# Two attention steps behind one logits stretch, a third room for turned keys and queries, and a state started one step earlier

## The chip, the cores and the metric

The kernel runs on one core of a Trainium2 chip. The metric is device time in microseconds, the median of several runs of one program. Engines are named PE (TensorE, with PEld for its weight loads), DVE (VectorE), ACT (ScalarE), POOL (GpSimd) and SP (SyncE, which issues the DMAs).

## What is computed

Three layers in a row, all in float32: retention attention over 8 batches, 8 heads, 576 positions and head size 64; a gated feed-forward layer over the 4608 tokens of width 512 (hidden width 2048); and a soft mixture of 8 experts with 4 slots each.

```python
scores = scale * np.matmul(q, k.transpose(0, 1, 3, 2))
gamma = 1.0 - 2.0 ** (-5.0 - np.arange(H, dtype=np.float32))
Dmat = np.where(rel >= 0, gamma[:, None, None] ** rel[None, :, :], 0.0)
x = np.matmul(scores * Dmat[None], v)              # attention, then heads side by side
...
h = x @ w_in
x = (h * (1.0 / (1.0 + np.exp(-1.702 * h)))) @ w_out
...
logits = x @ phi                                   # softmax over tokens: d, over slots: c
slot_out[e] = np.maximum((d.T @ x)[e] @ w1[e], 0.0) @ w2[e]
out = c @ slot_out
```

## The kernel before

**Attention steps.** A step g (0 to 35) is one chunk of 64 positions of two sequences for all eight heads; nine steps (NPB) finish a pair of sequences, and cb = g % 9 is the chunk's number. Attention is done in the chunked form: a running state St gathers keys times values, and the output of a chunk is its state times the queries plus its masked scores times its values. `products(g)` writes the step's TensorE work as 64x64 matmuls, two at a time for the lower and the upper half of the partitions. Its out products are 32 matmuls (SS with QT and VN with SC, into Op; 16 of them where cb is 0, since there is no state yet). Its own products are 16 for the state (KN with VN, into St; none where cb is 8) and 16 for the next step's scores (KT with QT of g + 1, into Sp). Own and out products are written alternately, so that one own pair and one out pair run side by side: a slot. DVE then makes SC out of Sp (`scale_scores`) and SS out of St (`scale_state`) for the next step, and xs out of Op (`scale_out`); ACT rounds xs into x (`x_high`), POOL takes the remainder (`x_low`) and scales the keys KN (`scale_keys`).

**Packs.** A step's turned keys KT, keys KN, turned queries QT and values VN come by one DMA of 1 MB into a pack, which also has room for SC and SS. From step 3 on two packs are used in turn, and `load_step(g + 2)` is issued at the end of step g.

**Blocks.** The feed-forward runs over 12 blocks of 384 tokens (three steps each), in 16 chunks fc of 128 hidden columns: `expert_scores` writes 12 matmuls into hp, ACT makes gT by a gelu, DVE transposes it into pre, SP shuffles pre by 16 small DMAs into nat. The second matrix of the feed-forward is folded into the logits: `logits_group` multiplies four chunks of gT with Wp into Lg. The softmax over tokens runs in pieces (`softmax_split` into Lp, `softmax_exp` with lt, `softmax_turn` with dp), and `slots_part` sums the slots (Sg).

**Order.** Every engine's queue is written by hand. The list START gives blocks 0 and 1 with steps 0 to 8. Blocks n = 2 to 10 are a loop, in which `step_of` puts the three steps of block n + 1 behind chunks 3, 9 and 13 of block n (12 for n = 9; chunks 0, 3 and 6 for n = 10); `between` puts logits groups of the block before behind the step of chunk 3, and of this block behind the step of chunk 9. So on TensorE the loop reads: chunk 3, a step, Lg, chunk 4, lt, chunks 5 and 6, dp, chunks 7 to 9, a step, Lg, Sg, chunks 10 to 13, a step, chunks 14 to 3 of the next block. After the last step the pool of packs closes (`att_ctx.close()`) and four rooms of 1 MB for expert weights open in its place (`pw2`); two expert units (`kept`) load in block 3 into rooms of `ring_raw`. Block 11 and the tail (expert layers and output) follow.

Of the kernel before, what the change touches and what calls it, by code (L numbers as in the profile page):

```python
# [9 lines left out]
F32 = mybir.dt.float32  # L10
# [8 lines left out]
B, H, S, D = 8, 8, 576, 64  # L19
# [7 lines left out]
C = 64  # L27
NPB = S // C
NP = H // 2
# [3 lines left out]
LAST = NBLK - 1  # L33
# [9 lines left out]
NSEQ = 2  # L43
CP = NSEQ * C
NSTEP = NT // CP
# [22 lines left out]
STEP_AT = {3: 0, 9: 1, 13: 2}  # L68
BEFORE_EARLY_STEP_AT = {3: 0, 9: 1, 12: 2}
LOGITS_AT = {3: ((1, 2), (1, 3)), 9: ((0, 0), (0, 1))}  # L70
SPLIT_AT, EXP_AT, TURN_AT, SLOTS_AT = 3, 4, 6, 9
EARLY_STEP_AT = {0: 0, 3: 1, 6: 2}
# [61 lines left out]
def tile_kernel(ctx, tc, qkv, w_in, w_turned, w_out, phi, w1, w2, consts, out):  # L134
# [42 lines left out]
    KT, KN, QT, VN, SC, SS = range(6)  # L177
# [3 lines left out]
    packs.update({g: packs[(g - 3) % 2] for g in range(3, NSTEP)})  # L181

    def load_step(g):
        sp.dma_start(packs[g].rearrange("p c a j d -> p (c a j d)")[:, 0:4 * PC], qkv[g])

# [11 lines left out]

    def products(g, parts=("out", "state", "score")):

        n, cb = g + 1, g % NPB  # L200
        own, out_ = [], []
        if "out" in parts and g >= 0:
            t = packs[g]
            Op = Ops[g] = ps.tile([128, NP, NSEQ, C], F32, tag="r", name="Op", bufs=3)
            for p, j in pairs:
                if cb:
                    out_.append((Op, t, SS, QT, p, j, True))
                out_.append((Op, t, VN, SC, p, j, cb == 0))
        if "state" in parts and g >= 0 and cb < NPB - 1:
            if cb == 0:  # L210
                St[g // NPB] = ps.tile([128, NP, NSEQ, D], F32, tag="St", name="St")
            own += [(St[g // NPB], packs[g], KN, VN, p, j, cb + p + j == 0) for p, j in pairs]
        if "score" in parts and n < NSTEP:
            Sp = Sps[n] = ps.tile([128, NP, NSEQ, C], F32, tag="r", name="Sp", bufs=3)
            own += [(Sp, packs[n], KT, QT, p, j, True) for p, j in pairs]
        for i in range(max(len(own), len(out_))):
            for what, turn in ((own, 0), (out_, 1)):
                if i < len(what):
                    o, w, a, b, p, j, first_ = what[i]
                    for h, oh in ((lo, (lo, hi)[turn]), (hi, (hi, lo)[turn])):  # L220
                        pe.matmul(o[oh, p, j, :], w[h, a, p, j], w[h, b, p, j], start=first_, stop=True,  # L221
                                  skip_group_check=True)
# [31 lines left out]
    def step_of(g, between):  # L254
        products(g)
        scale_keys(g + 1)
        scale_scores(g + 1)
        scale_state(g + 1)
        between()
        scale_out(g)  # L260
        x_high(g)
        x_low(g)
        if g + 2 < NSTEP:
            load_step(g + 2)
# [292 lines left out]
    def again():  # L557
# [11 lines left out]
        "A": products, "B": lambda i: products(i - 1, ("score",)), "P": lambda i: products(i, ("out", "score")),  # L569
# [247 lines left out]
    with tc.manual_schedule(engines={getattr(mybir.EngineType, e) for e in ("PE", "Activation", "DVE", "Pool", "SP")}):  # L817
        for x in START:
            step(x)
        for n in range(2, LAST):  # L820
# [3 lines left out]
                (STEP_AT if n < LAST - 2 else BEFORE_EARLY_STEP_AT, LOGITS_AT, SPLIT_AT, EXP_AT, TURN_AT, SLOTS_AT))  # L824
            for fc in range(NFC):
# [39 lines left out]
                if n == 3 and fc == 0:  # L865
                    for unit, a in zip(kept, (4, 8)):
                        load_unit(unit, lambda a=a, n=len(unit): ring_raw[:, a:a + 2 * n].rearrange("p a f -> p (a f)"))
# [76 lines left out]
```

## Time and profile before

| | |
|---|---|
| time, median of 3 runs | 653.29 us (652.22 to 653.52) |
| span of the profiled execution | 649.8 us |
| PE busy in it | 628.7 us, 97% |
| DVE, ACT, POOL busy | 292.9, 217.3, 77.8 us |
| DMA moved | 150.64 MB, mean 232 GB/s |

The span runs from the first to the last instruction of one profiled execution; the time of a run is some microseconds longer. Busy PE is modelled, since matmuls are pipelined: lengths of stretches are better taken as differences of starts. Each matmul of the code is two entries of PE in the profile, the feed-forward ones and those of lt excepted, which are one.

### The profile page before, as it was taken

To read this page: it belongs to the slowest core of one execution; us is meant where nothing else is said; L and a number is where in the kernel's file an instruction comes from. 1 tells how busy PE (TensorE), PEld (TensorE's weight loads), DVE (VectorE), ACT (ScalarE), POOL (GpSimd) and SP (SyncE) were. 2 spreads that over 40 slices of the span, in tenths; PEclk is the share of its full clock that TensorE was granted. 3 is DMA by queue.
4 is the path that set the end of the run, shared out by engine and by line. 5 is a ranking of instruction groups with operands and counts; after the bars stand their busy time and mean duration, and the time that the engine had idled before them with its cause. 6 is when DMAs were issued, how large, how long until landed. Compare 5 with 4: busy or idle time off the path is not lost.

```text
span 649.8 us, 19162 instructions
## 1 busy us (share of the span) xinstructions
PE 628.7 (97%) x8439; PEld 540.2 (83%) x8439; DVE 292.9 (45%) x581; ACT 217.3 (33%) x409; POOL 77.8 (12%) x70
## 2 busy tenths in 40 slices
PE   5999999999999999999999999999999999999994
PEld 5898887898989989989989979989898798874562
DVE  3989933463454443444534533534535323123043
ACT  2774432141242332412412412412424224231042
POOL 2021102111111102111111011111121100001000
PEclk9999999999999999999999999999999999999998
DMA  8987666886687647646566657466566778989998
GB/s 338 405 326 284 238 150 178 208 197 160 178 286 191 177 157 181 190 143 180 168 166 181 190 133 192 165 157 172 183 178 184 265 200 213 414 332 422 414 418 361
DMA packets 62546, 150.64 MB, mean 232 GB/s; under 512 B 8192, under 2 KB 42368, under 8 KB 53248
## 3 DMA queue, kind: packets, MB, share of 16 engines
q1 hardware_dynamic: 62464, 149.43, 72.3%
q8 instruction: 66, 1.08, 0.7%
q14 instruction: 16, 0.13, 0.1%
HBM read 101.16 MB, written 13.63 MB: 177 GB/s over the span
## 4 chain that ended last, share of the span: by engine, by line
PE 87%; DMA 5%; DVE 3%; ACT 2%; issue 1%; POOL 0%; SPq 0%; DVEq 0%; ACTq 0%
PE hp L359 56%; PE Lg L410 5%; PE Sg L470 4%; PE St L221 4%; PE Sp L221 4%; DMA early_raw<-in_moe_w_in_dram 3%; PE Op L221 3%; PE h_ps L701 2%; PE op L778 2%; PE so_ps L752 1%; DMA early_raw<-in_w_turned_dram 1%; PE so_ps L744 1%; DMA pack<-in_qkv_dram 1%; PE tpg L392 1%; DVE early_raw L299 1%
## 5 line engine op out<-in xcount | busy, mean ns | idle before, releaser
L359 PE MATMUL hp<-x,w 128*128 128x384 f32 x2304 | 420.0, 339 | 1.6 <-POOL x L251 1.3
L359 PEld LDWEIGHTS hp<-x,w 128*128 128x128 f32 x2304 | 397.4, 188 | 20.1 <-issue 15.7
L385 DVE STREAM_TRANSPOSE pre<-gT 128x384 f32<-128x384 f32 x172 | 95.3, 569 | 167.8 <-ACT gT L369 159.7
L369 ACT ACTIVATE gT<-hp 128x384 f32<-128x384 f32 x188 | 91.3, 491 | 229.9 <-PE hp L359 229.4
L251 POOL TENSOR_TENSOR x<-xs,x 128x512 fp32r<-128x512 f32 x33 | 42.6, 1290 | 319.0 <-ACT x L246 319.0
L221 PE MATMUL Op<-pack 64*64 64x64 f32 x2176 | 71.5, 220 | 0.6 <-issue 0.6
L221 PEld LDWEIGHTS Op<-pack 64*64 64x64 f32 x2176 | 66.4, 135 | 1.0 <-issue 1.0
L246 ACT CAST x<-xs 128x512 fp32r<-128x512 f32 x36 | 22.3, 620 | 87.2 <-DVE xs L239 87.2
L227 POOL TENSOR_TENSOR pack<-pack,cs 128x512 f32<-128x512 f32 x30 | 32.3, 1076 | 119.3 <-DMA pack<-in_qkv_dram 74.7
L221 PE MATMUL Sp<-pack 64*64 64x64 f32 x1152 | 40.9, 221 | 5.8 <-DMA pack<-in_qkv_dram 5.8
L221 PEld LDWEIGHTS Sp<-pack 64*64 64x64 f32 x1152 | 37.5, 137 | 7.4 <-DMA pack<-in_qkv_dram 5.8
L231 DVE TENSOR_TENSOR pack<-Sp,cs 128x512 f32<-128x512 f32 x36 | 24.7, 687 | 36.7 <-PE Sp L221 19.0
L221 PEld LDWEIGHTS St<-pack 64*64 64x64 f32 x1024 | 32.9, 136 | 8.2 <-issue 8.1
L221 PE MATMUL St<-pack 64*64 64x64 f32 x1024 | 37.3, 223 | 0.1
L410 PE MATMUL Lg<-gT,Wp 128*32 128x384 f32 x376 | 36.3, 493 | 0.6 <-DVE Lall L457 0.5
L470 PE MATMUL Sg<-nat,dn 128*32 128x512 f32 x264 | 30.4, 593 | 0.0
L239 DVE TENSOR_TENSOR xs<-Op,cs 128x512 f32<-128x512 f32 x36 | 24.5, 682 | 3.4 <-PE Op L221 3.4
L295 ACT ACTIVATE early_raw<-early_raw 128x512 f32<-128x512 f32 x28 | 18.9, 688 | 12.5 <-DMA early_raw<-in_w_turned_dram 7.5
L235 DVE TENSOR_TENSOR pack<-St,cs 128x512 f32<-128x512 f32 x32 | 21.8, 681 | 2.7 <-PE St L221 1.6
L470 PEld LDWEIGHTS Sg<-nat,dn 128*32 128x32 f32 x264 | 8.4, 110 | 17.1 <-issue 17.1
L476 DVE SCALAR_TENSOR_TENSOR acc<-acc,corr,Sg 128x512 f32<-128x512 f32 x10 | 7.5, 747 | 28.3 <-PE Sg L470 28.3
L410 PEld LDWEIGHTS Lg<-gT,Wp 128*32 128x32 f32 x376 | 9.6, 109 | 12.1 <-issue 9.1
(142 smaller groups left out, 385.5 us busy)
## 6 DMA issues: line engine op xcount, KB each, us to landing
pack<-in_qkv_dram SPq DMA_DIRECT2D x36, 1024.0 KB, 5.5
nat<-pre SPq DMA_DIRECT2D x352, 96.0 KB, 2.3
wx<-in_moe_w_dram SPq DMA_DIRECT2D x19, 1024.0 KB, 8.4
ring<-in_moe_w_out_dram SPq DMA_DIRECT2D x16, 512.0 KB, 3.7
early_raw<-in_moe_w_in_dram SPq DMA_DIRECT2D x15, 512.0 KB, 6.3
early_raw<-in_w_turned_dram SPq DMA_DIRECT2D x13, 512.0 KB, 7.8
wx<-in_moe_w_dram SPq DMA_DIRECT2D x11, 512.0 KB, 13.8
out_dram<-wx SPq DMA_DIRECT2D x5, 1024.0 KB, 6.1
```

Of the source, the lines that this page charges most:

```text
L221: pe.matmul(o[oh, p, j, :], w[h, a, p, j], w[h, b, p, j], start=first_, stop=True, skip_group_check=True)
L227: (dve if n in (3, 4) else pool).tensor_tensor(k, k, by_state(ksc[:, n % NPB, :]), op=ALU.mult)
L231: dve.tensor_tensor(packs[n][:, SC], Sps.pop(n), across(dtab), op=ALU.mult)
L235: dve.tensor_tensor(packs[n][:, SS], St[n // NPB], by_state(stsc[:, n % NPB, :]), op=ALU.mult)
L239: dve.tensor_tensor(xss[g], Ops.pop(g), across(osc), op=ALU.mult)
L246: act.copy(xh[b_][:, :, i * CP:(i + 1) * CP], xss[g].rearrange("p a j c -> p a (j c)"))
L251: (eng or pool).tensor_tensor(xl[b_][:, :, cols_], xss.pop(g).rearrange("p a j c -> p a (j c)"), xh[b_][:, :, cols_], op=ALU.subtract)
L359: pe.matmul(hp, wt[fc][:, a, dc, :], b[n][:, dc, :], start=(i == 0), stop=(i == 3 * NDC - 1))
L369: act.activation(gT[n, g][:, fl, :], hps.pop((n, fc)), AF.Gelu_apprx_sigmoid)
L385: dve.transpose(pre[n, hf][:, :, :, fh, :].rearrange("p c b i -> p (c b) i"), gT[n, g][:, fl, :].rearrange("p (x j) -> p x j", j=32))
L410: pe.matmul(Lg[n][32 * fl:32 * fl + 32, :], Wp[:, g * GF + fl, :], gT[n, g][:, fl, :], start=(g == 0), stop=(g == NFC // GF - 1))
L470: pe.matmul(Sg[32 * b:32 * b + 32], dn[n][:, c, :], nv[:, 4 * b:4 * b + 4], start=(c == 0), stop=(c == NT128 - 1))
```

## The change

The three steps of a block now stand in two places. Behind chunk 3 (chunk 0 in block 10), `two_steps` writes the first step, the logits groups, and the second step right behind them; behind chunk 9 (chunk 3 in block 10), `third_step` writes the third. For this, the scores of step g + 2 are computed while step g + 1's queries and step g's room are still in use, so the turned keys and queries get three rooms in rotation: those of the two packs and `third`, in `ring_raw[:, 8:10]`. A pack's load is split in two halves of 512 KB (`load_turned`, `load_natural`), and the input is laid out so that each half is contiguous. From step 8 on scores come ahead of the state among the own products, and the Sp buffer is taken ahead of Op. The state products of a step with cb = 0 (9, 18 and 27) are written into the step before it, which has no state products of its own. The kept unit that lay in `ring_raw[:, 8:10]` from block 3 on now loads in block 10, and the four rooms of `pw2` open behind chunk 3 of block 10 and not behind chunk 6.

```diff
-STEP_AT = {3: 0, 9: 1, 13: 2}
-BEFORE_EARLY_STEP_AT = {3: 0, 9: 1, 12: 2}
+STEP_AT = {3: 0, 9: 2}
...
-EARLY_STEP_AT = {0: 0, 3: 1, 6: 2}
+EARLY_STEP_AT = {0: 0, 3: 2}
...
-    KT, KN, QT, VN, SC, SS = range(6)
+    KT, QT, KN, VN, SC, SS = range(6)
...
+    third = ring_raw[:, 8:10].rearrange("p c (a j d) -> p c a j d", a=NP, j=NSEQ)
+
+    def turned_room(g):
+        if g < NPB:
+            return packs[g][:, 0:2]
+        return (packs[3][:, 0:2], third, packs[4][:, 0:2])[(g - NPB) % STEPS]
...
+    def load_turned(g):
+        if g < NSTEP:
+            sp.dma_start(turned_room(g).rearrange("p c a j d -> p (c a j d)"), qkv[g][:, 0:2 * PC])
+
+    def load_natural(g):
+        if g < NSTEP:
+            sp.dma_start(packs[g][:, 2:4].rearrange("p c a j d -> p (c a j d)"), qkv[g][:, 2 * PC:4 * PC])
...
+        if "state" in parts and g >= 0 and (g == 0 or 0 < cb < NPB - 1):
+            state = states(g)
+        elif "state" in parts and cb == NPB - 1 and 0 <= g < NSTEP - 1:
+            state = states(n)
+        if g < NPB:
+            new_scores()
+        own = state + score if g < NPB - 1 else score + state
...
-    def step_of(g, between):
+    def step_products(g, between):
         products(g)
-        scale_keys(g + 1)
         scale_scores(g + 1)
         scale_state(g + 1)
         between()
+
+    def step_x(g):
         scale_out(g)
         x_high(g)
         x_low(g)
-        if g + 2 < NSTEP:
-            load_step(g + 2)
+
+    def two_steps(g, between):
+        step_products(g, between)
+        products(g + 1)
+        step_x(g)
+        scale_scores(g + 2)
+        scale_state(g + 2)
+        step_x(g + 1)
+        load_natural(g + 2)
+        load_turned(g + 3)
+        load_natural(g + 3)
+        load_turned(g + 4)
+        scale_keys(g + 2)
+        scale_keys(g + 3)
+
+    def third_step(g, between):
+        step_products(g, between)
+        step_x(g)
+        load_natural(g + 2)
+        load_turned(g + 3)
+        scale_keys(g + 2)
...
                 if fc in step_at:
-                    step_of((n + 1) * STEPS + step_at[fc], between)
+                    (third_step if step_at[fc] else two_steps)((n + 1) * STEPS + step_at[fc], between)
...
+                    load_unit(kept[1], lambda: ring_raw[:, 8:10].rearrange("p a f -> p (a f)"))
```

PE, end of step 18 and what follows it, in block 5 (chunk 3). Names end in numbers that tell buffers apart; x2 is the lower and the upper half of one product. Before:

```order
L221 MATMUL St<-pack_93 64x64 x2
L221 MATMUL Op<-pack_93 64x64 x2
L221 MATMUL Sp<-pack_92 64x64 x16
L410 MATMUL Lg<-gT,Wp 32x384 x8
L359 MATMUL hp<-x,w 128x384 x12
L423 MATMUL lt<-Lp,sum4r 128x384 x2
```

After:

```order
L250 MATMUL Sp<-ring 64x64 x2
L250 MATMUL Op<-pack_92 64x64 x2
L459 MATMUL Lg<-gT,Wp 32x384 x8
L250 MATMUL Sp<-pack_93 64x64 x2
L250 MATMUL Op<-ring,pack_93 64x64 x2
```

The 16 unpaired Sp matmuls are gone, since the state products that stood beside Op are in step 17 and the scores stand there now; and step 19 begins right behind Lg, where chunk 4 stood.

DVE, around chunk 3 of block 6, from the transposes of the chunks ahead of it on. Before:

```order
L385 STREAM_TRANSPOSE pre<-gT 128x12x32 x5
L231 TENSOR_TENSOR pack_92<-Sp,cs 128x512
L235 TENSOR_TENSOR pack_92<-St,cs 128x512
L417 TENSOR_TENSOR Lp<-Lg,Lp 128x384
L239 TENSOR_TENSOR xs<-Op,cs 128x512
L385 STREAM_TRANSPOSE pre<-gT 128x12x32
L425 TENSOR_REDUCE mb<-lt 128x1
```

After:

```order
L434 STREAM_TRANSPOSE pre<-gT 128x12x32 x5
L260 TENSOR_TENSOR pack_92<-Sp,cs 128x512
L264 TENSOR_TENSOR pack_92<-St,cs 128x512
L466 TENSOR_TENSOR Lp<-Lg,Lp 128x384
L268 TENSOR_TENSOR xs<-Op,cs 128x512
L260 TENSOR_TENSOR pack_93<-Sp,cs 128x512
L264 TENSOR_TENSOR pack_93<-St,cs 128x512
L268 TENSOR_TENSOR xs<-Op,cs 128x512
L434 STREAM_TRANSPOSE pre<-gT 128x12x32
L474 TENSOR_REDUCE mb<-lt 128x1
```

SC, SS and xs of the second step now stand between xs of the first and the transpose of chunk 4.

SP, the loads of one block of the loop, from the weights' load ahead of chunk 3 on. Before:

```order
L281 DMA ring<-in_moe_w_out_dram 128x1024
L184 DMA pack_93<-in_qkv_dram 128x2048
L342 DMA wo_dram<-ring 128x512
L281 DMA ring<-in_moe_w_out_dram 128x1024
L184 DMA pack_92<-in_qkv_dram 128x2048
L403 DMA nat<-pre 32x3x256 x16
L184 DMA pack_93<-in_qkv_dram 128x2048
```

After:

```order
L330 DMA ring<-in_moe_w_out_dram 128x1024
L200 DMA pack_93<-in_qkv_dram 128x1024
L196 DMA pack_92<-in_qkv_dram 128x1024
L200 DMA pack_92<-in_qkv_dram 128x1024
L196 DMA ring<-in_qkv_dram 128x1024
L391 DMA wo_dram<-ring 128x512
L330 DMA ring<-in_moe_w_out_dram 128x1024
L200 DMA pack_93<-in_qkv_dram 128x1024
L196 DMA pack_93<-in_qkv_dram 128x1024
L452 DMA nat<-pre 32x3x256 x16
```

Three loads of 1 MB became six of 512 KB, four behind the pair and two behind the third step.

## Rows read from the trace of the kernel before

**Rows 1.** The page: head, and shares of the chain that ended last.

```profile
span 649.8 us, 19162 instructions
...
PE 87%; DMA 5%; DVE 3%; ACT 2%; issue 1%; POOL 0%; SPq 0%; DVEq 0%; ACTq 0%
```

**Rows 2.** Two blocks: stretch, length, busy by engine (instructions), clock, DMA share, GB/s.

```profile
296.58:342.71 46.13, 46.13 (x638) 41.33 (x637) 20.47 (x39) 14.58 (x27) 7.00 (x6) 1.00 0.62 172
...
250.47:296.58 46.11, 46.11 (x574) 41.31 (x573) 19.64 (x38) 14.69 (x27) 6.99 (x6) 1.00 0.63 173
```

**Rows 3.** Timeline of PE, one block: start, length, engine, line, operation, tiles, shapes, count.

```profile
298.61 12.75 PE L359 MATMUL hp<-x,w 128*128 128x384 f32 x72
311.29 0.27 PE L221 MATMUL St<-pack 64*64 64x64 f32 x2
...
313.32 1.50 PE L410 MATMUL Lg<-gT,Wp 128*32 128x384 f32 x16
314.75 2.38 PE L359 MATMUL hp<-x,w 128*128 128x384 f32 x12
316.97 0.51 PE L423 MATMUL lt<-Lp,sum4r 128*128 128x384 f32 x2
...
328.17 0.27 PE L221 MATMUL St<-pack 64*64 64x64 f32 x2
...
334.19 8.59 PE L359 MATMUL hp<-x,w 128*128 128x384 f32 x48
342.71 0.27 PE L221 MATMUL St<-pack 64*64 64x64 f32 x2
```

**Rows 4.** Timeline of PE, steps 17 (from 250.47) and 18 (from 265.18).

```profile
250.47 0.27 PE L221 MATMUL Sp<-pack 64*64 64x64 f32 x2
...
251.41 1.16 PE L221 MATMUL Op<-pack 64*64 64x64 f32 x34
252.50 12.75 PE L359 MATMUL hp<-x,w 128*128 128x384 f32 x72
265.18 0.27 PE L221 MATMUL St<-pack 64*64 64x64 f32 x2
...
266.16 1.10 PE L221 MATMUL Sp<-pack 64*64 64x64 f32 x32
267.19 1.50 PE L410 MATMUL Lg<-gT,Wp 128*32 128x384 f32 x16
```

**Rows 5.** Timeline of PE in the start: Lg ahead of a step, hp behind one.

```profile
59.61 0.85 PE L410 MATMUL Lg<-gT,Wp 128*32 128x384 f32 x8
60.39 0.27 PE L221 MATMUL St<-pack 64*64 64x64 f32 x2
...
93.69 2.35 PE L359 MATMUL hp<-x,w 128*128 128x384 f32 x12
95.88 0.49 PE L452 MATMUL dp<-ident,dT 128*128 128x128 f32 x3
```

**Rows 6.** Timeline of DVE around the step at 311.29; in brackets idle before, and releaser.

```profile
311.99 0.58 DVE L385 STREAM_TRANSPOSE pre<-gT 128x384 f32<-128x384 f32 x1 [1.56 <-ACT gT L369]
313.42 0.69 DVE L231 TENSOR_TENSOR pack<-Sp,cs 128x512 f32<-128x512 f32 x1 [0.86 <-PE Op L221]
314.03 0.68 DVE L235 TENSOR_TENSOR pack<-St,cs 128x512 f32<-128x512 f32 x1
```

**Rows 7.** Timelines of SP and POOL in block 3: a load and its keys.

```profile
179.97 0.64 SPq L184 DMA_DIRECT2D pack<-in_qkv_dram  x1
189.43 1.04 POOL L227 TENSOR_TENSOR pack<-pack,cs 128x512 f32<-128x512 f32 x1 [9.24 <-DMA pack<-in_qkv_dram]
```

**Rows 8.** Stretches of the last 120 us, columns as in rows 2.

```profile
530.00:550.00 20.00, 19.51 (x123) 17.30 (x123) 7.45 (x16) 8.37 (x15) 0.00 (x0) 1.00 0.75 187
...
580.00:640.00 60.00, 56.97 (x780) 31.11 (x781) 19.52 (x53) 17.10 (x41) 2.80 (x3) 1.00 1.01 408
640.00:650.00 10.00, 1.14 (x14) 0.87 (x9) 1.68 (x4) 1.16 (x4) 0.00 (x0) 0.69 0.77 316
```

More of the change, by code (lines that the diff above doesn't have):

```diff
@@ L181, in tile_kernel, with plane @@
     packs.update({g: packs[(g - 3) % 2] for g in range(3, NSTEP)})
+    third = ring_raw[:, 8:10].rearrange("p c (a j d) -> p c a j d", a=NP, j=NSEQ)
[3 more added lines that the diff above has]
+        return (packs[3][:, 0:2], third, packs[4][:, 0:2])[(g - NPB) % STEPS]
+    def plane(g, c):
+        return turned_room(g)[:, c] if c in (KT, QT) else packs[g][:, c]
     def load_step(g):
         sp.dma_start(packs[g].rearrange("p c a j d -> p (c a j d)")[:, 0:4 * PC], qkv[g])
+    def load_turned(g):
[4 more added lines that the diff above has]
+            sp.dma_start(packs[g][:, 2:4].rearrange("p c a j d -> p (c a j d)"), qkv[g][:, 2 * PC:4 * PC])
     St, Sps, Ops, xss = {}, {}, {}, {}
@@ L196, in tile_kernel, with states, new_scores @@
     pairs = [(p, j) for p in range(NP) for j in range(NSEQ)]
+    def states(g):
+        k = g // NPB
+        if k not in St:
+            St[k] = ps.tile([128, NP, NSEQ, D], F32, tag="St", name="St")
+        return [(St[k], g, KN, VN, p, j, g % NPB + p + j == 0) for p, j in pairs]
     def products(g, parts=("out", "state", "score")):
         n, cb = g + 1, g % NPB
-        own, out_ = [], []
+        out_, state, score = [], [], []
+        def new_scores():
+            if "score" in parts and n < NSTEP:
+                Sps[n] = ps.tile([128, NP, NSEQ, C], F32, tag="r", name="Sp", bufs=3)
+                score.extend((Sps[n], n, KT, QT, p, j, True) for p, j in pairs)
+        if g >= NPB:
+            new_scores()
         if "out" in parts and g >= 0:
-            t = packs[g]
             Op = Ops[g] = ps.tile([128, NP, NSEQ, C], F32, tag="r", name="Op", bufs=3)
@@ L206, in products @@
                 if cb:
[L207 to L215, printed above, removed]
+                    out_.append((Op, g, SS, QT, p, j, True))
+                out_.append((Op, g, VN, SC, p, j, cb == 0))
+        if "state" in parts and g >= 0 and (g == 0 or 0 < cb < NPB - 1):
[3 more added lines that the diff above has]
+        if g < NPB:
+            new_scores()
+        own = state + score if g < NPB - 1 else score + state
         for i in range(max(len(own), len(out_))):
@@ L220, in products @@
                     for h, oh in ((lo, (lo, hi)[turn]), (hi, (hi, lo)[turn])):
-                        pe.matmul(o[oh, p, j, :], w[h, a, p, j], w[h, b, p, j], start=first_, stop=True,
+                        pe.matmul(o[oh, p, j, :], plane(w, a)[h, p, j], plane(w, b)[h, p, j], start=first_, stop=True,
                                   skip_group_check=True)
@@ L568, in tile_kernel @@
         "ac": lambda i: join(f"O{i}", ring[:, i % 4]), "e": wp_product, "ed": wp_turn,
-        "A": products, "B": lambda i: products(i - 1, ("score",)), "P": lambda i: products(i, ("out", "score")),
+        "U": load_turned, "V": load_natural, "A": products, "B": lambda i: products(i - 1, ("score",)), "P": lambda i: products(i, ("out", "score")),
         "Q": lambda i: products(i, ("out",)), "R": lambda i: products(i, ("state",)),
@@ L823, in tile_kernel @@
                 (EARLY_STEP_AT, EARLY_LOGITS_AT, EARLY_SPLIT_AT, EARLY_EXP_AT, EARLY_TURN_AT, EARLY_SLOTS_AT) if early else
-                (STEP_AT if n < LAST - 2 else BEFORE_EARLY_STEP_AT, LOGITS_AT, SPLIT_AT, EXP_AT, TURN_AT, SLOTS_AT))
+                (STEP_AT, LOGITS_AT, SPLIT_AT, EXP_AT, TURN_AT, SLOTS_AT))
             for fc in range(NFC):
@@ L865, in tile_kernel @@
                 if n == 3 and fc == 0:
-                    for unit, a in zip(kept, (4, 8)):
-                        load_unit(unit, lambda a=a, n=len(unit): ring_raw[:, a:a + 2 * n].rearrange("p a f -> p (a f)"))
+                    load_unit(kept[0], lambda: ring_raw[:, 4:8].rearrange("p a f -> p (a f)"))
         n = LAST
@@ L930 @@
     q, k, v = inputs["q"], inputs["k"], inputs["v"]
-    side = lambda h: np.concatenate([turned(k, h), rows(k, h), turned(q, h), rows(v, h)], axis=2)
+    side = lambda h: np.concatenate([turned(k, h), turned(q, h), rows(k, h), rows(v, h)], axis=2)
     host = {"qkv": np.ascontiguousarray(np.concatenate([side(1), side(0)], axis=1)), **host}
```

4 rows, old and new, of the table START are left out of this document.

## The prediction

> **What bounds the kernel now.** The head of the page and its chain come first: of a span of 649.8 us the chain of waits gives 87% to PE and 5% to DMA [rows 1]. The table by stretches comes next. One block of the steady loop, from one third attention step to the next, takes 46.13 us, and PE is busy for all of it at a granted clock of 1.00, while VectorE has 20.47 us of work, ScalarE 14.58, GpSimd 7.00, and the DMA engines a share of 0.62 [rows 2]. So whatever leaves PE's row there leaves the span, as long as nothing else becomes late. The second row is the telling one: the block with steps 17 and 18 has 574 matmul entries instead of 638 and lasts 46.11 us [rows 2]. Sixty-four entries fewer bought nothing: in a step the reader must count slots, not matmuls. The PE timeline gives the lengths of all stretches as differences of starts [rows 3], and the two odd steps stand in [rows 4].
>
> **Part 1, the removed stretch.** Before, nine blocks (n = 2 to 10) enter attention three times; after, twice, and the second step stands between the logits Lg and the next feed-forward chunk. Feed-forward matmuls hp run at a fixed pace: 48 after Sg take 8.52 us up to the third step, 72 after that step 12.68 [rows 3], so 24 more cost 4.16, or 0.1733 each. Before, the stretch from Sg to the next block's first step is 8.52 + one step + 12.68, so 21.20 without the step. After, it is one run of 120: 8.52 + 72 x 0.1733 = 21.00. That returns 0.20. The moved step itself keeps its length. It now follows Lg: the only Lg followed by a step in the trace is in the start, eight entries in 60.39 - 59.61 = 0.78 us [rows 5]. Sixteen entries up to hp take 314.75 - 313.32 = 1.43 [rows 3]; eight more for 0.65, so the end of an Lg run costs 0.13 in both cases and the join costs nothing extra. The chunk after the pair now follows a step, not Lg: 12 such matmuls take 95.88 - 93.69 = 2.19 [rows 5] against 316.97 - 314.75 = 2.22 [rows 3], 0.03 more back. Sum: 0.23 x 9 = 2.1 us. Bounds: nothing, if Lg to step is dearer inside the loop, and 3.3 us if the whole entry and exit vanished (a step is 16 slots of 0.117, 1.87, in a stretch of 2.03 [rows 4], so 0.16, and with the 0.20 of the hp side 0.36 x 9). I take 2.1, because each of its terms has a row of the same neighbours.
>
> Changing from hp to a step shows as a gap: the last hp starts a step late by about half a pace. The Trainium skill, "TensorEngine Tiling (Array Packing)", Key Properties, says that changing the tiling mode drains TensorE. By that rule one counts changes of shape: eight in a block before, seven after, since Lg to step is still one. At 0.1 us each this would give 0.9 us in place of 2.1 and a time of 649.9. The rows are nearer to 2.1, because a change costs on both sides of it.
>
> **Part 2, the state one step early.** Step 17 ends in 34 unpaired Op entries, 251.41 to 252.50, step 18 in 32 unpaired Sp entries, 266.16 to 267.19 [rows 4]. Both steps last as long as a full one: 252.50 - 250.47 = 2.03 and 267.19 - 265.18 = 2.01 [rows 4]. The other steps pair every own product with an out product, 16 slots; at (2.03 - 0.16) / 16 a slot is 0.117 us. After, the 16 state matmuls of step 18 fill the empty half of step 17's slots at no time, and step 18 has 8 slots in place of 16: 8 x 0.117 = 0.93. The same holds for steps 8 and 9 and 26 and 27, so 3 x 0.93 = 2.8 us. Bound below: step 17 could grow, if paired slots were slower than single ones; [rows 4] excludes it, since paired halves and single halves have the same length.
>
> **Part 3, what the second step waits for.** It needs SC and SS of its own step, which VectorE makes out of the first step's products. Before, the first step starts at 311.29, the third chunk's transpose ends at 311.99 + 0.58 = 312.57, SC begins at 313.42 and SS ends at 314.03 + 0.68 = 314.71 [rows 6]. The second step would start where hp starts now, at 314.75 [rows 3]: in time by 0.04. After, scores come first in the slots, so SC can run while the state is still multiplied, and only SS remains for the time after the step; then 0.6 us are spare. In the shortened steps 9, 18 and 27 the second step starts 0.93 earlier: the transpose ends 1.28 after the step's start, SC and SS take 1.29 (313.42 to 314.71), so 2.57 plus some hundredths, against 2.03 - 0.93 + 1.43 = 2.53. I charge 0.1 for each, 0.3 in all; between 0 and 0.6. On VectorE the softmax's Lp stays ahead of the moved work. Queued behind that work are xs of both steps and the fourth chunk's transpose, and behind xs on ScalarE the gelu of the fourth chunk. These come later by the same 2.03 us as the chunk itself.
>
> **Part 4, loads and keys.** Each load of 1 MB becomes two halves; bytes stay. The natural half of step g+2 is issued after the pair's first step, then SP issues three more halves, and GpSimd scales g+2's keys (1.04 us) after two xl instead of one. The third step wants these keys in its second half: 2.03 + 1.43 + 2.03 + 2.19, then 328.17 - 316.97 = 11.20 for lt, five chunks and dp [rows 3], so 18.9 us after the first step's start, and 0.9 more. The slowest load of the loop was issued at 179.97 and its keys began at 189.43, 9.5 us later [rows 7]. From 5.5 us (the pair's length) that lands at 15, plus 1.04 for the keys: 16, against 19.8. Nothing is charged.
>
> **Part 5, the end.** DMA share is 1.01 from 580 to 640 and 0.77 after [rows 8], so the weights and outputs of the tail fill the DMA engines. But the stretch before has a share of 0.75 [rows 8]: there is no backlog going in, and each tail load waits for a room that PE empties. A PE that comes earlier pulls them along. The half megabyte of kept weights that now loads in block 10, and four rooms that fill three chunks earlier, fall into that open stretch. Nothing is charged.
>
> **The sum.** 2.1 + 2.8 - 0.3 = 4.6 us. The span of 649.8 becomes 645.2. The three runs have a median of 653.29, 3.5 above the span; this remainder is launch and end, which the change doesn't touch. So 648.7 us.
>
> **The rivals.**
> - Only the slots pay: the joins cost what the removed stretch returns, and SS is late in each pair. For it: 0.04 us of spare time before the reordering. Against it: [rows 5]. 2.8 - 0.3 = 2.5, so 650.8.
> - The tail holds the end: its DMA work doesn't move with PE, and the gain turns into waiting there. For it: 1.01 over 60 us [rows 8]. Against it: the open stretch before. It would give 652 to 653.3, no change.
> - More than the sum: the 0.36 per stretch of the upper bound, and one of the small stalls of block 2 gone. 2.1 becomes 3.3, no charge for SS: 6.1, so 647.2.
> - Slower: keys of the third step late. It decides when the natural half lands more than 13.3 us after issue (19.8 - 5.5 - 1.0); each microsecond beyond it stops PE in eight blocks (2 to 9). To eat 4.6 it takes 0.6 beyond, and at 14.7 it is 1.4 x 8 = 11.2, so 659.9. For it: two xl and three more loads are in the queues. Against it: 9.5 was the slowest of all [rows 7], and there a whole megabyte had to land. The Trainium skill, "DMA: Bandwidth & Descriptors", under its measured bandwidths, asks for at least 1 MiB in a DMA for three quarters of the peak, and the change halves that; with the loop at a share of 0.62 I leave this rival's chance small.
>
> **How the numbers follow.** Forecast 0.70 (647.7 to 649.9), only the slots 0.10, tail 0.08, more 0.08, slower 0.04. The range of 8 in 10 takes in the forecast, the slots alone and most of the upper case: 647.0 to 650.9. A difference of 0.2%, 1.3 us, is about what a measurement of this kernel can tell. Faster by that: 0.70 + 0.10 + 0.08 = 0.88; within it 0.08; slower 0.04.
>
> **What would show it.** In the profile after: a run of 120 hp at 21.0 us between Sg and the next step; blocks of about 45.9 us, and 45.0 where 9, 18 or 27 stands; these three steps at 1.1 us and steps 8, 17 and 26 still at 2.03; the second step starting 1.43 after Lg, except for about 0.1 in three blocks; keys ready before the third step. A gap on PE ahead of the second or third step would prove part 3 or 4 wrong, a PE that waits for DMA behind 580 us part 5.

## The result, and the profile after

The changed kernel takes 659.33 us against 652.79 for the kernel before, medians of six runs each on one chip: a ratio of 1.0097, with an interval of 1.0072 to 1.0122. So it is slower by 6.5 us, where the prediction said 4.6 us faster. The forecast range, 647.0 to 650.9 us, was missed. In the profiled executions the spans are 658.3 and 649.8 us, 8.5 apart. One run of a later kernel (884.28 us, at a granted clock of 0.66) is left out of that kernel's numbers.

Head and chain of the page after stand beside [rows 1]. PE has fallen from 87% of the chain to 84%, DMA has risen from 5% to 7%, and SP's queue has appeared:

```profile
span 658.3 us, 19183 instructions
...
PE 84%; DMA 7%; DVE 4%; ACT 2%; issue 1%; SPq 1%; POOL 0%; DVEq 0%; ACTq 0%
```

PE's waits over the whole span come next (engine, line of the waiting instruction, what was waited for; us in all, times, longest). Two of these rows are in the attention steps (L250), one in the slot sums, one in the feed-forward, and none of them was in the prediction:

```profile
PE St L250 <- issue: 2.6, 3, 2.0
PE Sg L519 <- DMA nat<-pre: 2.0, 1, 2.0
...
PE Op L250 <- issue: 1.4, 4, 0.5
...
PE hp L408 <- issue: 0.5, 1, 0.5
```

PE's timeline in block 3 shows what the joined stretch does (start, length, engine, line, operation, tiles, shapes, count; in brackets the idle time before it and its releaser):

```profile
157.32 21.07 PE L408 MATMUL hp<-x,w 128*128 128x384 f32 x120
178.32 0.27 PE L250 MATMUL Sp<-ring 64*64 64x64 f32 x2
...
180.35 1.50 PE L459 MATMUL Lg<-gT,Wp 128*32 128x384 f32 x16
...
184.35 0.33 PE L250 MATMUL Op<-pack 64*64 64x64 f32 x3 [0.50 <-issue]
184.61 0.61 PE L408 MATMUL hp<-x,w 128*128 128x384 f32 x2
```

The run of 120 lasts 178.32 - 157.32 = 21.00 us, to the hundredth the 21.00 forecast from [rows 3]. The first step lasts 2.03. The second one starts at 181.77, 1.43 behind Lg as forecast, and then lasts 184.61 - 181.77 = 2.84 instead of 2.03. Its loss is not at its head, where SS or keys would be waited for: three Op matmuls from its end, PE stands still and waits for nothing that the profile shows ("issue"). Seven of the nine second steps have such a stop, four of them at an Op and three at an St; the lengths of the nine are 2.57, 2.84, 2.80, 2.12, 2.43, 2.52, 4.34, 2.45 and 2.03 us, 5.9 us over nine times 2.03.

The second loss is in block 2. PE's timeline there, and two stretches of 1 us inside it (stretch, length, busy by engine with instructions, granted clock, DMA share, GB/s):

```profile
149.91 1.03 PE L519 MATMUL Sg<-nat,dn 128*32 128x512 f32 x4
152.93 4.46 PE L519 MATMUL Sg<-nat,dn 128*32 128x512 f32 x20 [1.98 <-DMA nat<-pre]
157.32 0.96 PE L408 MATMUL hp<-x,w 128*128 128x384 f32 x4
```

```profile
154.00:155.00 1.00, 1.00 (x8) 0.27 (x4) 1.00 (x2) 0.00 (x0) 0.00 (x0) 0.50 0.94 311
...
157.00:158.00 1.00, 1.00 (x6) 0.68 (x5) 0.57 (x1) 0.00 (x0) 0.70 (x1) 1.00 1.05 422
```

Sg, 2.69 us in every other block, lasts 7.41. It waits for the shuffle of block 1's second half, and when that has come, PE runs at a granted clock of 0.50, the level of 1.2 GHz, until 156 to 157 us. Of the 4.7 us lost the wait took 2.6 (the fifth matmul starts 3.02 us behind the first instead of 0.43) and the lower clock behind it 2.1. That the wait by itself lowers the clock is not shown: in e_shift below PE waited longer at this place and the clock stayed at 1.00.

The rest: the start was 1.5 us longer (step 9 at 128.04 against 126.52), and a chunk behind block 10's pair stopped for 0.8 (the last row of the waits above). In sum 5.9 + 4.7 + 1.5 + 0.8 = 12.9 us lost; with 8.5 us between the spans, 4.4 us of gains did come.

### The profile page after: what moved, and what is told of

Same layout as the page of the kernel before. It is cut to its first block, busy times and chain, and to the rows that moved or that the text cites. A ratio compares the mean times of both kernels' runs of the same rounds, so it can differ in the third digit from the quotient of the medians.

```text
span 658.3 us, 19183 instructions
## 1 busy us (share of the span) xinstructions
PE 629.8 (96%) x8439; PEld 539.9 (82%) x8439; DVE 294.5 (45%) x581; ACT 218.1 (33%) x409; POOL 78.3 (12%) x70
## 4 chain that ended last, share of the span: by engine, by line
PE 84%; DMA 7%; DVE 4%; ACT 2%; issue 1%; SPq 1%; POOL 0%; DVEq 0%; ACTq 0%
PE hp L408 53%; PE Lg L459 5%; PE Sg L519 5%; PE Sp L250 4%; DMA early_raw<-in_moe_w_in_dram 3%; PE Op L250 3%; PE St L250 3%; PE h_ps L750 2%; PE op L827 2%; DMA ring<-in_qkv_dram 2%; PE so_ps L801 1%; PE so_ps L793 1%; SPq L452 1%; DMA ring<-in_w_turned_dram 1%; DMA pack<-in_qkv_dram 1%
## 5 line engine op out<-in xcount | busy, mean ns | idle before, releaser
L250 PE MATMUL Op<-pack 64*64 64x64 f32 x1632 | 69.8, 220 | 1.2 <-issue 1.2
L250 PEld LDWEIGHTS Op<-pack 64*64 64x64 f32 x1632 | 62.0, 135 | 1.6 <-issue 1.6
L250 PEld LDWEIGHTS Sp<-pack 64*64 64x64 f32 x864 | 28.6, 139 | 14.3 <-DMA pack<-in_qkv_dram 5.6
L250 PE MATMUL St<-pack 64*64 64x64 f32 x1024 | 37.2, 222 | 2.6 <-issue 2.6
L250 PEld LDWEIGHTS St<-pack 64*64 64x64 f32 x1024 | 33.7, 138 | 5.1 <-issue 4.4
L250 PE MATMUL Sp<-pack 64*64 64x64 f32 x864 | 32.2, 225 | 5.6 <-DMA pack<-in_qkv_dram 5.6
L519 PE MATMUL Sg<-nat,dn 128*32 128x512 f32 x264 | 33.1, 620 | 2.0 <-DMA nat<-pre 2.0
```

The costliest lines, as they stand in the source:

```text
L250: pe.matmul(o[oh, p, j, :], plane(w, a)[h, p, j], plane(w, b)[h, p, j], start=first_, stop=True, skip_group_check=True)
L519: pe.matmul(Sg[32 * b:32 * b + 32], dn[n][:, c, :], nv[:, 4 * b:4 * b + 4], start=(c == 0), stop=(c == NT128 - 1))
```

## The experiments

The first theory for the second step: PE's instructions arrive in pieces, and two steps close together use them up faster than they come. The profile has a queue for them (queue, kind: packets, MB, share), in the page after:

```profile
q8 instruction: 66, 1.08, 0.7%
```

All 66 packets have 16,384 bytes. PE has 17,019 records in this trace (8439 matmuls, 8439 weight loads, 138 waits, 3 drains), so a packet is about 256 instructions of 64 bytes. Counting PE's records from the start of the span shows where the stops fall (written out from the records of three kernels; the gap is from the start of the matmul before to the start of the stopped one, the last column is how long before that start the last of these packets had landed; of e_shift and e_dose two rows each):

```
kernel          start us  gap ns  record   modulo 256   landed before
changed           132.94     436    4290          194            1.30
changed           184.35     714    5570          194            1.34
changed           231.06     677    6850          194            1.28
changed           321.56     363    9154          194            1.45
changed           367.95     399   10434          194            1.39
changed           416.20    2208   11714          194            1.42
changed           462.57     380   12994          194            1.29
changed           506.96     844   14274          194            1.36
e_shift           185.74     553    5569          193            1.37
e_shift           326.94     580    9409          193            1.50
e_dose            169.16    1593    5314          194            1.52
e_dose            490.56    1877   16066          194            1.39
```

The row at 506.96 is the chunk behind block 10's pair: by the count it is the same kind of stop, so this cause took 6.7 us in this execution, not 5.9.

The same in a view of the profile: from stop to stop, PE's matmuls and PEld's weight loads (second and third counts) with the nine waits between them that this view leaves out make 1280, five times 256, in the changed kernel:

```profile
184.35:231.06 46.71, 46.25 (x635) 41.56 (x636) 20.15 (x39) 14.71 (x27) 6.92 (x7) 1.00 0.68 193
...
321.56:367.95 46.40, 46.22 (x635) 41.52 (x636) 20.80 (x41) 14.71 (x27) 6.98 (x6) 1.00 0.63 172
```

The rivals are VectorE (SS or SC late), keys late on GpSimd, and loads late because they are smaller. VectorE can be read off the trace after, where it is tightest, in block 8 with its short first step:

```profile
410.92 0.69 DVE L260 TENSOR_TENSOR pack<-Sp,cs 128x512 f32<-128x512 f32 x1
411.53 0.68 DVE L264 TENSOR_TENSOR pack<-St,cs 128x512 f32<-128x512 f32 x1
```

```profile
412.25 0.27 PE L250 MATMUL Sp<-pack 64*64 64x64 f32 x2
```

SS ends at 412.21, the second step starts at 412.25, and its stop of 2.2 us comes at 414 to 416, long after. For the others, runs.

**Shift the count.** The changed kernel, with matmuls that do nothing put in early:

```diff
-... t16 t17 A6 t18 ...
+... t16 t17 X32 A6 t18 ...     # X32: 32 matmuls of 64x64 by 32 columns into an unused tile
```

> The changed kernel with 32 small matmuls into a spare tile (128 records on PE: 64 matmuls and 64 weight loads) put in early, before step 6; they cost about 1 us and change nothing else. Theory (instruction supply): PE's program comes in pieces of 256 instructions (16,384 bytes), and the stalled matmul is the first of a piece that has not come. All nine stalls of the pairs stand at one place in the count of PE's records (194 modulo 256); with 128 records more they must stay at 194 of the new count, so each falls on a matmul 128 earlier or later in the program, and the sizes change places: blocks 3 and 4, now 0.81 and 0.77 us, to about 0.4; blocks 6 and 7, now 0.41 and 0.50, to about 0.7. Rivals (the second step waits for SC or SS from VectorE, for keys from GpSimd, or for its loads): the same matmuls of the program stall by the same times, whatever was counted before them.

One run, 662.67 us; the added matmuls took 3.6 us, not 1. The stops stand at 193 of the new count in all six cases, so in the program they have moved. In block 3 the matmul that stood still three Op from the end of the step now runs on time, and the stop is 1.5 us into the step:

```profile
185.74 0.27 PE L250 MATMUL Op<-pack 64*64 64x64 f32 x2 [0.34 <-issue]
```

The second steps of blocks 3 and 4 now last 2.68 and 2.55 us, 0.65 and 0.53 too long, where it had been 0.81 and 0.77; those of blocks 6 and 7 are 0.59 and 0.85 too long, before 0.41 and 0.50. Block 8's stop of 2.2 us is gone (2.12 us for the step), and block 5, which had none, has one of 1.9. The sizes alone would prove nothing: in a second profile of the unshifted kernel, below, block 3's step is only 0.28 too long and block 6's 0.80. The places do: no data that a step waits for knows how many instructions went before. This decides against all three rivals.

Block 2's Sg takes 6.15 us here. Its wait is longer than in the changed kernel, and the clock behind it (first column behind POOL, in the second fence) stays at 1.00:

```profile
157.10 2.77 PE L519 MATMUL Sg<-nat,dn 128*32 128x512 f32 x20 [2.42 <-DMA nat<-pre]
```

```profile
158.00:159.00 1.00, 1.00 (x14) 0.40 (x8) 1.00 (x3) 0.00 (x0) 0.00 (x0) 1.00 1.01 287
```

**The dose, without the change.** The kernel before, with part of each single step issued twice:

```diff
-        products(g)
+        products(g, again=True)     # out and score products once more, behind the first
```

> The kernel before, in which each of the 27 single steps of the blocks issues its output and score products a second time, right behind the first (192 records of PE more, 128 in steps 9, 18 and 27; the results are written again with the same values). Nothing new is waited for. At the pace of a step (256 records in 2.03 us) this is 24 x 1.52 + 3 x 1.01 = 39.5 us, so by the rivals (a second step waits for data) 692 us, and no matmul inside a step is late. Theory (instruction supply): a run of 448 records at this pace has two beginnings of 256-record pieces in it in three cases of four, and the second is late by 0.4 to 1.2 us: some 20 stalls, 8 to 24 us more, 700 to 716 us, and each stalled matmul stands at one place in the count of records modulo 256.

720.24 us, 67.9 more than the kernel before (652.35). The longer step lasts 3.89 us where nothing stops it, 1.87 more than the single one, not 1.52: half of the second issue's Op matmuls are unpaired and take a slot of their own, as in [rows 4]. That is 24 x 1.87 + 3 x 0.93 = 47.7 us without a stop. In nine of 27 steps PE stands still; these are 12.4 us too long in sum. PE's waits of this kernel have eight of them in one row, with a stop of 0.5 us in the start, and the ninth in another:

```profile
PE Op L222 <- issue: 9.8, 9, 1.7
...
PE Sp L222 <- issue: 0.5, 1, 0.5
```

Four more stops stand at 193 or 194 modulo 256 as well, in the Lg right behind a step (242.28, 313.91, 402.00 and 473.56 us), 1.4 to 1.5 us after a packet landed. They make the Lg, or Lg and Sg together, 0.7 to 1.0 us too long, 3.5 in sum:

```profile
402.00 0.53 PE L415 MATMUL Lg<-gT,Wp 128*32 128x384 f32 x4 [0.18 <-issue]
```

So neither the joined stretch nor anything else of the change is needed: one run of some 450 dense records is enough. Fewer places were hit than I expected (13, not some 20), and harder, by 0.7 to 1.9 us. The start was 3.9 us longer in this execution, though nothing in it is changed. With it the sum is 47.7 + 12.4 + 3.5 + 3.9 = 67.5 of the 67.9 us.

**The pair with something slow inside.** The changed kernel with the pair at chunk 9, where logits and slot sums can both stand between the two steps. In this kernel steps 17 and 26 read the next sequence's first keys and values before these are loaded, so it counts for its time alone.

```diff
-STEP_AT = {3: 0, 9: 2}
+STEP_AT = {3: 0, 9: 1}              # step 0 alone; steps 1 and 2 joined
...
         step_products(g, between)
+        step_x(g)
+        slots()                     # Sg and the shuffle behind it
         products(g + 1)
-        step_x(g)
```

> The changed kernel with the pair put elsewhere: step 0 of a block alone at chunk 3, steps 1 and 2 in one stretch at chunk 9, with the logits and the slot sums (Sg, 24 records of 512 columns, 2.7 us) between them; single steps in block 10. The stretch holds 256 + 32 + 48 + 256 records of PE, but 256 in a row now last 3.2 us at least only where they take in all of the logits, and above 5 us where they take in Sg. Theory (instruction supply): second steps of 2.03 to 2.1 us, no stall, and the gains of both parts stay: 652.8 - 2.8 - 8 x 0.23 = 648.2 us. Rival (SC and SS or the ring of PSUM rooms hold the second step): a gap ahead of the second step, not inside it, 0.3 us or more in each of 8 blocks, 650.5 us or above. Rival (any second step close behind a first stalls, since it is the sum of both that counts): second steps of 2.4 to 2.8 us, 652 us.

The second steps of blocks 3 to 8 last 2.03 us each, without a stop; those of blocks 2 and 9 lose 0.13 and 0.33 (the latter at 193 modulo 256). So a second step close behind a first is not slow as such: it is slow when 256 instructions run off faster than the next ones come. Yet the time is 653.94 us, 1.0024 of the kernel before, with an interval of 1.0008 to 1.0040: none of the three times expected, and 5.7 us above the theory's. Block 2's Sg again waited (4.79 us), and the run of 120 behind the pair was slower as a whole:

```profile
245.99 21.46 PE L409 MATMUL hp<-x,w 128*128 128x384 f32 x120
...
267.38 0.27 PE L250 MATMUL Sp<-ring 64*64 64x64 f32 x2
```

21.39 us instead of 21.00, in six blocks alike (3 to 8; block 2 has 21.00). Each matmul takes 176.6 ns on average instead of 173.3, from the first to the last. This takes back more than the removed stretch gives: the block from 197.63 to 243.97 lasts 46.34 us, [rows 2] 46.11 to 46.13.

**The shuffle ahead of the loads.**

```diff
         load_natural(g + 2)
         load_turned(g + 3)
+        if g // STEPS == 3:
+            shuffle(1, 1)
         load_natural(g + 3)
         load_turned(g + 4)
...
-                if fc == (0 if early else min(step_at)) and (early or n == 2):
+                if fc == (0 if early else min(step_at)) and early:
```

> The changed kernel, with block 2's second shuffle (shuffle(1, 1), 16 DMAs on SP) put ahead of the last two of the pair's four loads. Theory (order on SP): the shuffle landed late only because it stood behind loads that wait for the second step; Sg of block 2 falls from 7.41 us to about 2.7 us and the time by 4.7 us, to 654.6 us. Rival (the moved loads themselves keep the DMA engines or the semaphores of SP's transfers busy, wherever they stand): Sg stays above 5 us and the time stays at 659 us. The stalls inside the second steps stay as they were, 5.9 us in sum, by both.

654.73 us, 1.0042 of the kernel before (1.0026 to 1.0058): the time of the theory, but only in part by its way. Sg of block 2 still lasts 4.26 us, with a shorter wait and no drop of the clock (1.00 over all of it); and the second steps lose 2.2 us in sum in this profile, not 5.9.

**Three single steps again.** The joined stretch undone, all else kept:

```diff
-STEP_AT = {3: 0, 9: 2}
-EARLY_STEP_AT = {0: 0, 3: 2}
+STEP_AT = {3: 0, 9: 1, 13: 2}        # 12 in block 9
+EARLY_STEP_AT = {0: 0, 3: 1, 6: 2}
```

> The changed kernel with the joined stretch undone: three single steps at chunks 3, 9 and 13 (12 in block 9; 0, 3 and 6 in block 10) as before, each followed by its own two half loads and its keys; the third room, the new order of the planes in the input and the state one step early stay. Theory (instruction supply and the order on SP): both losses go, and what is left is the state: 652.8 - 2.8 = 650.0 us, single steps 2.03 us, Sg of block 2 2.7 us. Rival (the smaller loads, the third room or the new input layout cost time by themselves): above 651.5 us. Rival (the start, 1.5 us later at step 9 in the one profile of the changed kernel, is slower for good): 651.5 us.

All stops in the steps are gone; single steps last 2.03 us, steps 9, 18 and 27 1.09. The time is 651.89 us, 0.9994 of the kernel before (0.9977 to 1.0011), by its number what the rivals said. The missing 1.9 us against 650.0 are for the most part in one row: Sg of block 2 lasts 4.41 us, 1.72 too long. Here SP issues the last piece of the shuffle at 144.0 us, 2.4 later than before (141.6). So the order on SP is still the likelier reading than smaller loads as such; what stands ahead of the shuffle is shown under part 4 below.

**The changed kernel and the kernel before once more**, for second profiles:

> The changed kernel once more, unchanged, for a second profile. Theory (instruction supply): the stalls of the second steps stand at 194 modulo 256 again, but their sizes differ from the first profile (they hang on when a piece of the program arrives), 3 to 6 us in sum; block 2's Sg is 7.4 us again. Rival (VectorE, keys or loads late): the same stalls by the same times. The start up to step 9 is anywhere from 126.5 to 128 us.

> The kernel before once more, unchanged, for a second profile of its start: the time up to step 9 was 126.52 us in its first profile and 128.04 in that of the changed kernel. If the start of the changed kernel is slower for good, this one is at 126.5 again; if the start differs between executions, it is anywhere from 126.5 to 128.

The changed kernel took 656.93 us in this run. Six stops, all at 194 again, but with other sizes: the second step of block 2 now 4.15 us, that of block 3 2.30, of block 8 4.06; 6.4 us in sum. And Sg of block 2 lasts 2.69 us: the stop of 2.1 us ahead of it gave the shuffle the time that it lacked. So the two losses are not independent, and the 7.41 us of the first profile are not in every execution. In this one the clock fell elsewhere: behind the stops of blocks 2 and 8, both near 2 us, it was 0.50 for some 3 us, and the feed-forward there took 3.0 us longer in sum (the chunk behind block 2's pair 3.28 us instead of 2.19). The kernel before took 651.92 us and reached step 9 at 126.35 us.

**The order of the planes alone.**

```diff
-    KT, KN, QT, VN, SC, SS = range(6)
+    KT, QT, KN, VN, SC, SS = range(6)
```

> The kernel before with the new order of the four planes alone (turned keys, turned queries, keys, values, in the input and in the packs); nothing else is moved. Up to step 9 the four profiles of unshifted kernels with this order took 126.85 to 128.04 us, the three without it 126.35 to 126.52. Theory (the order of the planes makes the start slower): 126.9 us or more at step 9, and 0.5 to 1.5 us more in all, 653 to 654 us. Rival (chance, or another part of the change that stands in the start): 126.4 us, and 652.4 us.

652.90 us, 0.9998 of the kernel before (0.9979 to 1.0017): no difference. Its profile, though, reaches step 9 at 128.66 us. So the start differs from execution to execution: in the five profiles of kernels with the old order step 9 comes at 126.35, 126.39, 126.52, 126.88 and 130.42 us (the last one in e_dose), in the six with the new order, e_shift left out, at 126.85 to 128.66. Only e_dose has the old order that late; without it the two groups touch only at 126.85 to 126.88. So the profiles decide neither way, and the 1.5 us that I put down as a loss of the start may be chance or not; the times say no difference, to about 1.3 us.

**The state one step early alone**, on the kernel before:

```diff
+        s = n if cb == NPB - 1 and g < NSTEP - 1 else g
-        if "state" in parts and g >= 0 and cb < NPB - 1:
+        if "state" in parts and g >= 0 and (g == 0 or s % NPB < NPB - 1 and (s > g or cb > 0)):
...                                    # KN and VN of step s; its keys are scaled behind its load
```

> The kernel before with one part of the change alone: the states of a sequence's first chunk (16 of its matmuls) are computed one step early, in steps 8, 17 and 26, and its keys are scaled early for that; no joined stretch, no third room, no half loads, no new order in the input. Theory: the gain of part 2 is real and nothing is lost with it, steps 9, 18 and 27 take 1.09 us instead of 2.01, 652.5 - 2.8 = 649.7 us. Rival (steps 8, 17 and 26 become longer by what the others lose): 652.5 us.

650.13 us, 0.9962 of the kernel before (0.9948 to 0.9976). Steps 9, 18 and 27 last 1.09 us, steps 8, 17 and 26 still 2.03, Sg of block 2 2.69. This is the fastest of all these kernels, faster than both that were compared. Its chain of waits:

```profile
span 646.6 us, 19162 instructions
...
PE 87%; DVE 6%; DMA 3%; ACT 2%; issue 1%; POOL 0%; DVEq 0%; ACTq 0%
```

**Another stretch removed, with few instructions.** On top of the last one, dp is moved from chunk 6 to the front of the step at chunk 9:

```diff
+                if fc == slots_at and not early:
+                    softmax_turn(n - 1)
                 if fc in step_at:
...
-                if fc == turn_at:
+                if fc == turn_at and early:
```

> The kernel with the states one step early alone, and one stretch joined that asks for few instructions: the turn of the softmax (dp, 6 records of PE) is moved from chunk 6 to the front of the step at chunk 9, ahead of the step, the logits and the slot sums, so that eight blocks have one stretch less between products. Theory (a stretch less is worth what part 1 said, and only the dense second step cost more): no stall inside the step, 0.2 to 0.25 us in each of 8 blocks, 1.8 us less than the states alone, 0.9935 of the time before, 648.3 us. Rival (the sums wait for dn, which VectorE now makes 8 us later): Sg starts late, 0.5 us or more in each of 8 blocks, 652 us. Rival (a stretch less is worth nothing by itself): 650.1 us.

652.98 us, the median of eleven runs, 1.0011 of the kernel before (0.9991 to 1.0030). PE's timeline of a block in the middle:

```profile
230.10 10.57 PE L363 MATMUL hp<-x,w 128*128 128x384 f32 x60
240.51 0.49 PE L456 MATMUL dp<-ident,dT 128*128 128x128 f32 x3
240.93 0.27 PE L222 MATMUL St<-pack 64*64 64x64 f32 x2
...
246.96 8.74 PE L363 MATMUL hp<-x,w 128*128 128x384 f32 x48
255.63 0.27 PE L222 MATMUL St<-pack 64*64 64x64 f32 x2
```

Chunks 5 to 9 and dp take 240.93 - 230.10 = 10.83 us; apart, in the kernel with the state alone, they took 4.17 + 0.25 + 6.43 = 10.85. So the price of a removed stretch is 0.02 here, not 0.2: what hp no longer pays at two borders, dp pays at its new one with the step (0.42 from dp's first matmul to the step, where it had been 0.25 to hp). And the run of 48 takes 8.67 us, not 8.52: again all of its matmuls at 176.6 ns. In the profiled execution, at 656.4 us one of the slower ones, block 2 adds a wait of 4.0 us of Lg for VectorE, which had the turn's sums behind other work (rival two, in one block and in another place than it said), and behind it Sg runs at a granted clock of 0.50 for some 3 us and takes 4.38 us.

## Why the prediction was wrong

**Where it was right.** Part 2 came out, and the lengths that part 1 worked with. The run of 120 hp is 21.00 us; the second step starts 1.43 behind Lg; the chunk behind the pair takes 2.18 (2.19 in part 1). Steps 9, 18 and 27 take 1.09 us (1.1 forecast), steps 8, 17 and 26 stay at 2.03: part 2 is worth 2.8 us in the trace, and alone 2.2 us between the medians. The charge of part 3 for steps 9, 18 and 27, 0.1 each, is what block 5's second step shows, 2.12. Part 5 held too: PE's last 96 hp started 8.45 us later than before and the span ended 8.5 later, so the end moved with PE. A slip of no weight: the sum adds 3.5 us for launch and end, but in the runs on record the time is only some 1.9 us above the span of the same execution.

**Part 3 failed.** It asked what data the second step waits for and found SC and SS. It never asked whether PE gets its instructions. By the trace, a single step's 256 records run off in 2.03 us; where the count then passes the border of a piece, PE goes on 3.01, 3.28, 3.58, 3.63 or 3.48 us after it passed the border before (5.04 in block 8; 2.38 in block 2, where the packet was under way before that border). A step between chunks doesn't show this, since 256 records of hp last 22 us and the next packet has long landed; the second step follows too soon. Of those 3 us and more the packet's own transfer is 0.9 to 1.6 us, and every stopped matmul of a second step started 1.26 to 1.56 us after its packet had landed. The stops cost 5.9 us in the second steps and 0.8 in a chunk, and the prediction's sum has no term for them. The Trainium skill, "Runtime: NRT & Kernel Launch", Instruction fetch mechanics, has the blocks of 16 KiB and 256 instructions, fetched one ahead, and calls their cost mostly hidden; the trace agrees on the size, but not on the cost.

The trace of the kernel before had shown it. In the start, where steps 0 to 2 run without a break, PE stops once in the middle:

```profile
13.31 0.27 PE L221 MATMUL Op<-pack 64*64 64x64 f32 x3 [0.60 <-issue]
```

That matmul stands at 193 modulo 256 as well. It was the only place in the program that resembled the joined stretch, and of the start the prediction used the price of Lg to step alone [rows 5].

What sets the size of a stop is open in part. It differs from execution to execution: 2.2, 5.9 and 6.4 us in sum in three profiles with the same order on PE. In three of the four longest stops of the changed kernel's two profiles and e_shift (block 8 twice, block 5 of e_shift) the packet began only 2.0 to 2.7 us after PE had passed the border before, in the short stops of the second steps at most 1.5 us after it. Why it began late was not tried. The data moved on the DMA engines doesn't explain it alone: 0.7 to 1.0 MB in the 4 us before those four, 0.4 to 0.5 before the short ones, but four of the nine stops in e_dose's steps, 1.0 to 1.6 us, had less than 0.1.

**Part 4 failed for another reason than the one it weighed.** It worked out when the loads land and when keys are ready, and those were in time: the rival of late keys, which was the one for slower, did not happen, and that its 659.9 us lies near the measured 659.33 is luck. What it left out is that other work stands behind the loads on SP. In block 2 that is the shuffle of 16 transfers, which in the kernel before follows one load and now follows four. SP's timelines before and after (start, length, line, tiles, count):

```profile
113.32 2.53 SPq L403 DMA_DIRECT2D nat<-pre  x4
...
128.25 13.94 SPq L403 DMA_DIRECT2D nat<-pre  x16
```

```profile
116.85 0.33 SPq L200 DMA_DIRECT2D pack<-in_qkv_dram  x1
...
117.84 12.26 SPq L452 DMA_DIRECT2D nat<-pre  x16
...
133.27 0.33 SPq L200 DMA_DIRECT2D pack<-in_qkv_dram  x1
133.64 0.47 SPq L196 DMA_DIRECT2D ring<-in_qkv_dram  x1
134.21 16.75 SPq L452 DMA_DIRECT2D nat<-pre  x16
```

Its first piece was issued 1.7 us behind step 9's start before (128.25 - 126.52) and 6.2 after (134.21 - 128.04). Two of the four loads use rooms of the second step, as the theory of e_shuffle had it, but from 118 us on SP waited only 0.3 us for PE at these loads. Two other things weigh more. First, the list START was changed too: two new loads (V10 and U11) stand in it ahead of the shuffle of block 1's first half, and SP waits at the first of them for step 8 (SP's waits after, 100 to 119 us):

```profile
SPq L200 <- PE Op L250: 7.7, 1, 7.7
```

So that shuffle begins at 117.84 us and not at 113.32, and what stands behind it on SP comes later. Second, the shuffle itself lasts longer, since its pieces wait for loads to land, 5.7 us against 2.5 (SP's waits during it, before and after):

```profile
SPq L403 <- DMA pack<-in_qkv_dram: 2.5, 1, 2.5
```

```profile
SPq L452 <- DMA pack<-in_qkv_dram: 4.1, 3, 2.1
SPq L452 <- DMA ring<-in_qkv_dram: 1.6, 1, 1.6
```

The runs agree: in e_shuffle and e_apart the first piece is issued 4.8 us behind step 9, and Sg still takes 4.26 and 4.41 us; both have the changed START. e_state has the old one, and 2.69 us. No run put START's loads back alone, so the share of each is not measured.

**Part 1 was too dear by a quarter, and its rule too general.** The terms that it lists came out, but it left out that hp has two paces. Behind the moved step, the 24 hp between lt and dp run at 176.6 ns and not 173.9, and take 4.24 instead of 4.17 us. Without its stop a block takes 45.95 us instead of 46.12: about 0.17 of the 0.23. And e_dp9 shows that a removed stretch is worth nothing where the parts that come together pay at their new border. Counting changes of tile shape, the other view in part 1, fits that run: hp, dp and the step have as many of them before as after, since hp and dp are both 128x128.

**The chances.** Slower had 0.04, for one mechanism. Each new wait had been weighed by its own spare time, but not what the new order asks of things that the trace of before never showed under stress: the supply of instructions, and a queue with more ahead of an old transfer.

## What to carry to other kernels

Before two dense runs of small matmuls are put close together, count records: here 256 of them (a matmul and its weight load are two) needed some 3 us from piece to piece, and an "issue" wait inside a run that waits for nothing is the sign; counted from the start, all stops then stand at one value modulo 256. Of work that is moved on a queue, list what stands behind it in each block, also in the one block where the order is special. And take the parts of a change one by one: here the state one step early alone is 0.4% faster, and the joining cost more than twice that (1.0097 of the kernel before, against 0.9994 with single steps).

## What the runs showed of the hardware

- PE's instructions come in packets of 16,384 bytes (66 in the changed kernel, 86 in the one with doubled products), and a dense run can outrun them: seven of nine second steps stopped at a border, for 0.4 to 2.2 us from matmul to matmul.
- A long run of hp matmuls has one of two paces from its start to its end, 173.3 or 176.6 ns a matmul (21.00 or 21.39 us for 120), with the same instructions and the same granted clock of 1.00. Runs at one place of the block mostly had the same pace in all blocks of a kernel, but not always (e_pair9: 21.00 us in block 2, 21.39 in six others). What decides it was not tried.
- After a PE stop of about 2 us or more the granted clock fell to 0.50, the level of 1.2 GHz, for about 3 us in some cases: in Sg of the changed kernel, behind two stops of its second profile, and in e_dp9. In others it stayed at 1.00: behind the stop of 2.2 us in block 8 of the changed kernel, and behind the longer wait in e_shift's Sg. What decides is not shown. Behind stops of 0.4 to 0.9 us in second steps, and waits of 0.5 to 1.1 us in Sg, it stayed at 1.00.
